# A ring of three tiles for v, loads held back, and no scores at the end of an h stage, in a fused attention and MLP kernel

## The chip, the cores and the metric

The kernel runs on one core of one Trainium2 chip. The metric is the device time of one execution in microseconds. Every time below is from runs on the chip; the engines are called PE (matmuls), ACT (activations), DVE (vector work), POOL (here the issuer of loads) and SP (the issuer of transposes and stores).

## What is computed

The reference, cut to what matters:

```python
batch, n_heads, seq, head_dim = 8, 12, 448, 64        # q, k, v
n_tokens, d_model, d_ff = 3584, 768, 2048             # w_in, w_out
scores = q @ k.T / sqrt(64) - log(448)
attn   = sigmoid(scores)                              # no softmax: no sums over rows
x      = (attn @ v), heads side by side               # 3584 x 768
h      = x @ w_in
out    = (h * sigmoid(h)) @ w_out
```

Inputs and output are float32 in HBM; the kernel works in float16 with float32 sums.

## The kernel before, in words

**Attention.** The 12 heads of a batch are worked four at a time, so there are 3 groups per batch and 24 groups g in all; group g belongs to batch g // 3. A group's q, k and v are loaded by `load` (L72): one tile [128, 2, 7, 64] float16 per tensor, in two transfers of 112 KB each, issued by POOL and converted from float32 on the way. Tiles come from rings: four for k, four for q, five for v. The load of a tile waits until the tile that had the slot before has been read by all its users, and POOL issues in program order, so a waiting load holds up all later ones.

q and k are needed transposed (`kT`, `qT`, rings of four). Groups 0 to 5 are transposed on PE (`pe_transpose`, L141). From group 6 on `dma_transpose` (L160) first copies the tile into rows (`kr`, `qr`; by ACT for groups 6 to 8, by DVE later), and SP then issues a DMA that transposes. `scores(g, ch)` (L171) does four 64x64 matmuls into one of two PSUM tiles `psc` and one sigmoid on ACT; seven of them make a group. `values(g)` (L195) does 28 matmuls with the group's v into two PSUM tiles `pav`, and DVE scales these into `xT`.

**MLP.** `h_unit(b, fc)` (L229) is one of 16 column blocks of a batch: six matmuls into a PSUM tile `ph`, a sigmoid on ACT (`tsig`), a product on DVE (`gTr`). 16 of them are an h stage. `out_set` (L286) makes two row blocks of the output with seven products of eight matmuls each instead of eight (sums and differences of the operands, `S1` to `S4` and `T1` to `T4`, are prepared on DVE). Its first product needs `gTr` of the lower eight column blocks, its second that of the upper eight, its third a difference of two blocks.

`ph`, `pav`, `po` (the products) and PE's transposes share a ring of four PSUM tiles, `ps_1`.

**Order.** The order is written by hand. `all_moe` (L376) is one long stream of MLP steps, each with a cost in ns (189 for a matmul of h, 163 for one of a product). The main loop takes two `scores` at a time ("a burst"), then `values` if a group is complete, then a row copy for a later group if one is due (`rows_if_any`), and then `stretch(ns)` (L395), which draws steps from the stream until their costs reach all that was granted so far. The grant per burst is 1600 to 3400 ns. Before burst 42 (group 6, first chunk) there is one long `stretch(21500)`, with no scores in it: the rest of batch 0's h stage, all of batch 1's and the start of the first `out_set`. In batch 1's h stage `by_h1` (L351) places the row copies and transposes of groups 6, 7 and 8 behind column blocks 4, 7 and 10, each followed by the loads of k and q four groups on.

Loads beside the first ones are issued from `after_transpose` (L425), `after_values` (L443), `by_h1` and `rows_if_any` (L461). `w_in` comes in four quarters (column blocks 4 to the quarter), `w_out` in four parts.

Of the kernel before, what the change touches and what calls it, by code (L numbers as in the profile page):

```python
# [17 lines left out]
def kernel(  # L18
# [21 lines left out]
    NFC = DFF // P  # L40
    NO2 = DMODEL // 2
    NQB = NQ * B
# [7 lines left out]
    p2 = ctx.enter_context(tc.tile_pool(name="p2", bufs=2))  # L50
    p3 = ctx.enter_context(tc.tile_pool(name="p3", bufs=3))
    p4 = ctx.enter_context(tc.tile_pool(name="p4", bufs=4))
    p5 = ctx.enter_context(tc.tile_pool(name="p5", bufs=5))
    p12 = ctx.enter_context(tc.tile_pool(name="p12", bufs=12))
    ps_sc = ctx.enter_context(tc.tile_pool(name="ps_sc", bufs=2, space=bass.MemoryType.PSUM))
    ps_1 = ctx.enter_context(tc.tile_pool(name="ps_1", bufs=4, space=bass.MemoryType.PSUM))
# [8 lines left out]
    flat = {}  # L65

    def new_flat(name, g):
        flat[name, g] = (p5 if name == "v" else p4).tile(
            [P, 2, NCH, D], F16, tag=f"{name}f", name=f"{name}f"
        )  # L70

    def load(names, g, c0=0, c1=NCH):  # L72
        b, iq = divmod(g, NQ)
        for name in names:
            if (name, g) not in flat:
                new_flat(name, g)
            for half in range(2):
                h0 = half * (H // 2) + 2 * iq
                nc.gpsimd.dma_start(  # L79
                    flat[name, g][half * HP : (half + 1) * HP, :, c0:c1].rearrange(  # L80
                        "p i c d -> p i (c d)"
                    ),
                    source[name][b, h0 : h0 + 2].rearrange("i (p c) d -> p i (c d)", c=NCH)[
                        :, :, c0 * D : c1 * D
                    ],
                )
# [20 lines left out]
    def load_w_in(step):  # L107
        cols = slice(step * DFF // 4, (step + 1) * DFF // 4)
        nc.gpsimd.dma_start(  # L109
            w_in_sb[:, :, cols], moe_w_in[:, cols].rearrange("(cc p) f -> p cc f", p=P)  # L110
        )

    def load_w_out(nh, part):
        cols = slice(nh * NO2, (nh + 1) * NO2)
        fcs = slice(part * NFC // 2, (part + 1) * NFC // 2)
        nc.gpsimd.dma_start(
            w_out_sb[:, fcs, cols],
            moe_w_out[part * DFF // 2 : (part + 1) * DFF // 2, cols].rearrange(
                "(fc p) e -> p fc e", p=P
            ),  # L120
        )
# [104 lines left out]

    pairs = [half * NQ + iq for iq in range(NQ - 1) for half in range(2)] + [NQ - 1, 2 * NQ - 1]

    def h_unit(b, fc):  # L229
        ph = ps_1.tile([P, 512], F32, tag="ps1", name="ph")  # L230
        for at, cc in enumerate(pairs):
            assert b in ready or at < 4
            nc.tensor.matmul(  # L233
                ph[:, :S],
                w_in_sb[:, cc, fc * P : (fc + 1) * P],
                xT[b][:, cc, :],
                start=(at == 0),
                stop=(at == NCC - 1),
            )
            if at < NCC - 1:  # L240
                yield 189
        if fc == NFC - 1:
            h_done.add(b)
        tsig = p3.tile([P, S], F16, tag="tsig", name="tsig")
        nc.scalar.activation(tsig, ph[:, :S], AF.Sigmoid, bias=0.0, scale=ISX)  # L245
        nc.vector.tensor_mul(  # L246
            gTr[:, fc, (b % 2) * S : (b % 2) * S + S], ph[:, :S], tsig
        )
        yield 189
# [34 lines left out]
        return [rows_of[2 * m + u // NCH, u % NCH] for u in (2 * g, 2 * g + 1)]  # L284

    def out_set(a1, rows1, a2, rows2, last=False):  # L286
        lo, hi = slice(0, NHC), slice(NHC, NFC)
        osb = [p4.tile([P, DMODEL], F32, tag="osb", name="osb") for _ in range(2)]
        c11, c12 = (osb[0][:, nh * NO2 : (nh + 1) * NO2] for nh in range(2))
        c21, c22 = (osb[1][:, nh * NO2 : (nh + 1) * NO2] for nh in range(2))  # L290
        m1 = p2.tile([P, NO2], F32, tag="m1", name="m1")
        sg = [cpool.tile([P, NHC, P], F16, tag=f"S{i}", name=f"S{i}") for i in range(1, 5)]

        def store(rows, o, cols, engines):
            for at, (row, eng) in enumerate(zip(rows, engines)):
                eng.dma_start(row[:, cols], o[at * HP : (at + 1) * HP, cols])

        left, right, whole = slice(0, NO2), slice(NO2, DMODEL), slice(0, DMODEL)

        def product(a, w):  # L300
            po = ps_1.tile([P, 512], F32, tag="ps1", name="po")
            for fc in range(NHC):
                nc.tensor.matmul(  # L303
                    po[:, :NO2], a[:, fc, :], w[:, fc, :], start=(fc == 0), stop=(fc == NHC - 1)
                )
                if fc < NHC - 1:
                    yield 163
            return po[:, :NO2]

        def plus(o, po, x, sign=ISX):  # L310
            nc.vector.scalar_tensor_tensor(  # L311
                out=o, in0=po, scalar=sign, in1=x, op0=ALU.mult, op1=ALU.add
            )

        nc.vector.tensor_sub(sg[2], a1[:, lo], a2[:, lo])  # L315
        nc.vector.tensor_add(sg[0], a2[:, lo], a2[:, hi])
        po = yield from product(a1[:, lo], wq[0][0])
        nc.scalar.activation(m1, po, AF.Copy, scale=ISX)  # L318
        nc.vector.tensor_sub(sg[1], sg[0], a1[:, lo])
        yield 163  # L320
        po = yield from product(a1[:, hi], wq[1][0])
        plus(c11, po, m1)
        nc.vector.tensor_sub(sg[3], a1[:, hi], sg[1])
        if last:
            store(rows1, osb[0], left, (nc.sync, nc.sync))
        yield 163
        po = yield from product(sg[2], tw[3])
        plus(c22, po, m1)
        yield 163
        po = yield from product(sg[1], tw[2])  # L330
        plus(c22, po, c22)
        plus(c12, po, m1)
        yield 163
        po = yield from product(a2[:, hi], tw[4])
        plus(c21, po, c22, -ISX)
        yield 163
        po = yield from product(sg[0], tw[1])
        plus(c22, po, c22)
        plus(c12, po, c12)
        store(rows2, osb[1], whole, (nc.sync, nc.sync))  # L340
        yield 163
        po = yield from product(sg[3], wq[1][1])
        plus(c12, po, c12)
        if last:
            store(rows1, osb[0], right, (nc.sync, nc.scalar))
        else:
            store(rows1, osb[0], whole, (nc.sync, nc.sync))
        yield 163


    by_h1 = {4: 6, 7: 7, 10: 8}  # L351
    early = [h_unit(0, fc) for fc in range(2)]
    sums = w_sums()

    def moe_h(b):
        for fc in range(NFC):
            yield from early[fc] if b == 0 and fc < 2 else h_unit(b, fc)
            if b == 1:
                if fc >= 2:
                    next(sums)  # L360
                if fc in by_h1:
                    for name in ("k", "q"):
                        dma_transpose(by_h1[fc], name, act_copy)
                    load("kq", by_h1[fc] + 4)

    def moe_set(m, g):
        step = out_set(block(g), row_blocks(m, g), block(g + 1), row_blocks(m, g + 1))
# [25 lines left out]
    done = due = 0.0  # L393

    def stretch(ns):  # L395
        nonlocal done, due
        due += ns
        while done < due:
            step_ns = next(stream, None)
            if step_ns is None:  # L400
                break
            done += step_ns
# [19 lines left out]
    units = [(g, ch) for g in range(NQB) for ch in range(NCH)]  # L422
    waiting = []

    def after_transpose(g):  # L425
        if g == 0:
            load("kq", 4)
            load_w_in(1)
        elif g == 1:
            load("kq", 5)  # L430
            load_w_in(2)
            load("v", 3)
            load_w_in(3)
            load("v", 4)
        elif g == 4:
            load("kq", 8)
            load("v", 6)
            load("v", 7)
        elif g == 5:
            load("v", 8)  # L440
            load("kq", 9)

    def after_values(g):  # L443
        if g == 0:
            load("v", 5)
            for nh in range(2):
                for part in range(2):
                    load_w_out(nh, part)
        elif g == 2:
            load("kq", 6)  # L450
            load("kq", 7)
        elif g >= 4 and g + 5 < NQB:
            load("v", g + 5)
        if g >= 6:
            for to in (9, 10) if g == 6 else (g + 4,):
                if to < NQB:
                    later.extend(((to, "k"), (to, "q")))

    later = []

    def rows_if_any():  # L461
        if later:
            g, name = later.pop(0)
            dma_transpose(g, name, nc.vector.tensor_copy)
            if name == "q" and g + 4 < NQB:
                load("kq", g + 4)

    def values_if_any():
# [110 lines left out]
```

## Time and profile before

| what | value |
| --- | --- |
| median of three runs | 386.41 us (384.43, 386.41, 386.48) |
| the profiled execution | 386.89 us |
| its span, first to last instruction | 385.1 us |
| around the span | 1.79 us |
| busy share of ACT, DVE, POOL | 62%, 61%, 24% |
| loads (POOL's queue) | 22.69 MB |
| stores and transposes (SP's queue) | 19.31 MB |

The share of busy time is an average over the whole span. PE's busy time counts matmuls whose ends are modelled, so what is worth looking for is not the share but the places at which PE had nothing to run, and what released it. In a line of the timeline the first number is the start in us from the span's start, the second the length of the run of instructions merged into that line, xN their count, and the bracket at the end the idle time of the engine ahead of it with its releaser. In a view of windows the columns are the stretch, its length, busy time of PE, PE's weight loads, DVE, ACT and POOL (counts in parentheses), the granted clock of PE, the busy share of the DMA engines and GB/s moved.

### The profile page before, as it was taken

What the parts mean: (1) busy time and instruction counts of PE and PEld (TensorE: products, weight loads), DVE (VectorE), ACT (ScalarE), POOL (GpSimd) and SP (SyncE); (2) the same over time, 40 slices, a digit from 0 to 9 for tenths busy, and PEclk for the clock granted to TensorE, in tenths of its full rate; (3) what the DMA queues carried; (4) which work ended last, traced back from release to release, by engine and by line L of the source; (5) the groups of instructions that cost most, each with busy time, mean ns of one, the idle gap of its engine ahead of it and who ended that gap; (6) DMA issues with size and microseconds to landing.
All of it is one profiled execution on the core that took longest, in us unless ns stands there. A gap on an engine that the chain in (4) does not pass through costs nothing.

```text
span 385.1 us, 7662 instructions
## 1 busy us (share of the span) xinstructions
PE 373.2 (97%) x3083; PEld 186.8 (48%) x3083; DVE 233.5 (61%) x415; ACT 240.1 (62%) x328; POOL 93.0 (24%) x158
## 2 busy tenths in 40 slices
PE   7998999997999999999999999999999999999995
PEld 2543445553544444444555444544455444555663
DVE  2445646894685656655767546745757444756774
ACT  4998685856766886678454587577874686044000
POOL 8953516541344313221312301101000000000000
PEclk9999999999999999999999999999999999999999
DMA  7999999999999999928949764445131300110233
GB/s 111 181 190 205 205 203 170 153 130 119 195 108 210 147 212 112 171 53 98 98 107 201 68 137 73 39 115 73 24 69 40 83 3 0 26 57 2 67 98 82
DMA packets 66403, 42.71 MB, mean 111 GB/s; under 512 B 37056, under 2 KB 62912, under 8 KB 66368
## 3 DMA queue, kind: packets, MB, share of 16 engines
q0 software_dynamic: 28032, 22.69, 45.0%
q1 hardware_dynamic: 38112, 19.31, 30.1%
q8 instruction: 24, 0.39, 0.4%
q10 hardware_dynamic: 224, 0.23, 0.2%
q14 instruction: 11, 0.09, 0.1%
HBM read 45.61 MB, written 11.01 MB: 147 GB/s over the span
## 4 chain that ended last, share of the span: by engine, by line
PE 83%; DMA 8%; ACT 5%; POOL 1%; issue 1%; DVE 1%; ACTq 0%; POOLq 0%
PE ph L233 36%; PE po L303 31%; PE psc L178 9%; PE pav L209 7%; ACT attnT L185 5%; DMA qT<-qr 4%; DMA vf<-in_v_dram 3%; DMA kf<-in_k_dram 1%; POOL qf L79 1%; DVE gTr L246 0%; ACT tsig L245 0%; PE ptrk L149 0%; POOL w_in_sb L109 0%; DVE S L315 0%; POOL vf L79 0%
## 5 line engine op out<-in xcount | busy, mean ns | idle before, releaser
L185 ACT ACTIVATE attnT<-psc,bias_s 128x896 f16<-128x896 f32 x168 | 159.1, 1015 | 57.7 <-PE psc L178 57.7
L233 PE MATMUL ph<-xT,w_in_sb 128*128 128x448 f16 x768 | 153.6, 353 | 0.0
L246 DVE TENSOR_TENSOR gTr<-ph,tsig 128x448 f16<-128x448 f32 x128 | 78.1, 623 | 75.3 <-ACT tsig L245 74.5
L233 PEld LDWEIGHTS <-w_in_sb 128*128 128x128 f16 x768 | 71.8, 98 | 76.2 <-issue 13.6
L245 ACT ACTIVATE tsig<-ph 128x448 f16<-128x448 f32 x128 | 68.2, 545 | 49.9 <-PE ph L233 49.0
L303 PEld LDWEIGHTS <-S 128*128 128x128 f16 x448 | 42.1, 98 | 34.5 <-issue 6.7
L79 POOL DMA_DIRECT2D vf<-in_v_dram x48 | 28.7, 615 | 104.7 <-PE pav L209 98.2
L311 DVE SCALAR_TENSOR_TENSOR osb<-po,osb 128x384 f32<-128x384 f32 x70 | 37.7, 555 | 26.7 <-PE po L303 26.1
L178 PE MATMUL psc<-qT,kT 64*64 64x448 f16 x672 | 50.4, 362 | 3.5 <-DMA qT<-qr 2.1
L220 DVE TENSOR_SCALAR xT<-pav 128x448 f16<-128x448 f32 x48 | 27.7, 620 | 30.9 <-PE pav L209 30.9
L303 PE MATMUL po<-T,S 128*128 128x384 f16 x224 | 40.7, 327 | 0.5 <-DVE S L315 0.5
L303 PEld LDWEIGHTS <-gTr 128*128 128x128 f16 x304 | 28.8, 98 | 23.5 <-issue 4.3
L303 PE MATMUL po<-w_out_sb,S 128*128 128x384 f16 x224 | 39.9, 326 | 0.0
L209 PE MATMUL pav<-attnT,vf 64*64 64x448 f16 x672 | 38.3, 350 | 1.7 <-DMA vf<-in_v_dram 1.2
L79 POOL DMA_DIRECT2D qf<-in_q_dram x48 | 28.8, 611 | 35.6 <-DVE qr L164 10.9
L303 PE MATMUL po<-w_out_sb,gTr 128*128 128x384 f16 x192 | 34.4, 326 | 0.2 <-DVE gTr L246 0.2
L79 POOL DMA_DIRECT2D kf<-in_k_dram x48 | 28.7, 606 | 20.5 <-DMA w_out_sb<-in_moe_w_out_dram 6.1
L178 PEld LDWEIGHTS <-kT 64*64 64x64 f16 x672 | 14.9, 104 | 34.1 <-issue 33.1
L209 PEld LDWEIGHTS <-vf 64*64 64x64 f16 x672 | 20.2, 107 | 14.0 <-DMA vf<-in_v_dram 1.9
L311 DVE SCALAR_TENSOR_TENSOR osb<-po,m 128x384 f32<-128x384 f32 x42 | 23.2, 552 | 3.5 <-PE po L303 3.1
L303 PE MATMUL po<-T,gTr 128*128 128x384 f16 x112 | 21.4, 326 | 0.0
L318 ACT ACTIVATE m<-po 128x384 f32<-128x384 f32 x14 | 6.9, 493 | 21.4 <-PE po L303 21.4
(40 smaller groups left out, 131.0 us busy)
## 6 DMA issues: line engine op xcount, KB each, us to landing
out_dram<-osb SPq DMA_DIRECT2D x54, 192.0 KB, 3.4
qf<-in_q_dram POOLq DMA_DIRECT2D x48, 112.0 KB, 7.3
vf<-in_v_dram POOLq DMA_DIRECT2D x48, 112.0 KB, 4.7
kf<-in_k_dram POOLq DMA_DIRECT2D x46, 112.0 KB, 7.6
w_in_sb<-in_moe_w_in_dram POOLq DMA_DIRECT2D x4, 768.0 KB, 10.8
w_out_sb<-in_moe_w_out_dram POOLq DMA_DIRECT2D x4, 768.0 KB, 15.3
kT<-kr SPq DMA_TRANSPOSE x18, 7.5
qT<-qr SPq DMA_TRANSPOSE x18, 7.0
```

Of the source, the lines that this page charges most:

```text
L79: nc.gpsimd.dma_start(flat[name, g][half * HP : (half + 1) * HP, :, c0:c1].rearrange("p i c d -> p i (c d)"), source[name][b, h0 : h0 + 2] ...
L178: nc.tensor.matmul(psc[own, j, :S], qkT["k", g][rows, ch, own], qkT["q", g][rows, :, own], start=True, stop=True,)
L185: nc.scalar.activation(attnT[g, ch], psc[:, :, :S], AF.Sigmoid, bias=bias_s, scale=QKSCALE)
L209: nc.tensor.matmul(pav[half][j * D : (j + 1) * D, :S], flat["v", g][own, j, ch, :], at[own, j, :], start=(ch == 0), stop=(ch == NCH - 1),)
L220: nc.vector.tensor_scalar_mul(xT[b][:, half * NQ + iq, :], pav[half][:, :S], SX)
L233: nc.tensor.matmul(ph[:, :S], w_in_sb[:, cc, fc * P : (fc + 1) * P], xT[b][:, cc, :], start=(at == 0), stop=(at == NCC - 1),)
L245: nc.scalar.activation(tsig, ph[:, :S], AF.Sigmoid, bias=0.0, scale=ISX)
L246: nc.vector.tensor_mul(gTr[:, fc, (b % 2) * S : (b % 2) * S + S], ph[:, :S], tsig)
L303: nc.tensor.matmul(po[:, :NO2], a[:, fc, :], w[:, fc, :], start=(fc == 0), stop=(fc == NHC - 1))
L311: nc.vector.scalar_tensor_tensor(out=o, in0=po, scalar=sign, in1=x, op0=ALU.mult, op1=ALU.add)
L318: nc.scalar.activation(m1, po, AF.Copy, scale=ISX)
```

## The change

It has four parts.

1. v's ring has three tiles instead of five. The load of v for group g+3 now stands behind `values(g)` throughout. v of group 3 (the first of batch 1) is issued ahead of the third quarter of `w_in`; v of group 4 behind the fourth quarter; v of group 5 between the halves of `w_out`.
2. The loads of v of groups 9 and 10 and of k and q of groups 10 to 12 are held: v of group 9 and then k and q of groups 10, 11 and 12, which hung on `by_h1`, are issued behind `values(6)`; v of group 10 follows `values(7)`. k and q of group 9 stand behind `values(5)`. From group 10 on the row copies of a group stand behind `values` of the group three earlier; before, it was four.
3. `by_h1` goes from blocks 4, 7, 10 to blocks 3, 6, 9.
4. `hold`: from the start of the last column block of an h stage (of any batch but 0) to the end of the first product of an `out_set`, `stretch` draws on beyond its grant, so that no burst falls into that stretch. What was drawn too much is drawn less in the next stretches.

```diff
-        flat[name, g] = (p5 if name == "v" else p4).tile(
+        flat[name, g] = (p3 if name == "v" else p4).tile(
...
     def h_unit(b, fc):
+        nonlocal hold
+        hold = b > 0 and fc == NFC - 1
...
         po = yield from product(a1[:, lo], wq[0][0])
         nc.scalar.activation(m1, po, AF.Copy, scale=ISX)
         nc.vector.tensor_sub(sg[1], sg[0], a1[:, lo])
+        hold = False
         yield 163
...
-    by_h1 = {4: 6, 7: 7, 10: 8}
+    by_h1 = {3: 6, 6: 7, 9: 8}
...
                     for name in ("k", "q"):
                         dma_transpose(by_h1[fc], name, act_copy)
-                    load("kq", by_h1[fc] + 4)
...
-        while done < due:
+        while done < due or hold:
...
     def after_transpose(g):
         if g == 0:
             load("kq", 4)
             load_w_in(1)
         elif g == 1:
             load("kq", 5)
-            load_w_in(2)
-            load("v", 3)
-            load_w_in(3)
-            load("v", 4)
         elif g == 4:
             load("kq", 8)
-            load("v", 6)
-            load("v", 7)
-        elif g == 5:
-            load("v", 8)
-            load("kq", 9)

     def after_values(g):
         if g == 0:
+            load("v", 3)
+            load_w_in(2)
+            load_w_in(3)
+        elif g == 1:
+            load("v", 4)
+            load_w_out(0, 0)
+            load_w_out(0, 1)
+        elif g == 2:
             load("v", 5)
-            for nh in range(2):
-                for part in range(2):
-                    load_w_out(nh, part)
-        elif g == 2:
+            load_w_out(1, 0)
+            load_w_out(1, 1)
             load("kq", 6)
             load("kq", 7)
-        elif g >= 4 and g + 5 < NQB:
-            load("v", g + 5)
-        if g >= 6:
-            for to in (9, 10) if g == 6 else (g + 4,):
-                if to < NQB:
-                    later.extend(((to, "k"), (to, "q")))
+        elif g + 3 < NQB:
+            load("v", g + 3)
+        if g == 6:
+            for to in (10, 11, 12):
+                load("kq", to)
+        if g == 5:
+            load("kq", 9)
+        if g >= 6 and g + 3 < NQB:
+            later.extend(((g + 3, "k"), (g + 3, "q")))
...
-            if name == "q" and g + 4 < NQB:
+            if name == "q" and g + 4 < NQB and g + 4 > 12:
                 load("kq", g + 4)
```

More of the change, by code (lines that the diff above doesn't have):

```diff
@@ L52 @@
     p4 = ctx.enter_context(tc.tile_pool(name="p4", bufs=4))
-    p5 = ctx.enter_context(tc.tile_pool(name="p5", bufs=5))
     p12 = ctx.enter_context(tc.tile_pool(name="p12", bufs=12))
@@ L286, in out_set @@
     def out_set(a1, rows1, a2, rows2, last=False):
+        nonlocal hold
         lo, hi = slice(0, NHC), slice(NHC, NFC)
@@ L319, in out_set @@
         nc.vector.tensor_sub(sg[1], sg[0], a1[:, lo])
+        hold = False
         yield 163
```

## The prediction

> **What bounds the kernel now.** I read the page first, then PE's waits, then PE's timeline at the places that the waits name, then POOL's and SP's timelines behind them, and the DMA in windows.
>
> ```profile
> span 385.1 us, 7662 instructions
> PE 373.2 (97%) x3083; PEld 186.8 (48%) x3083; DVE 233.5 (61%) x415; ACT 240.1 (62%) x328; POOL 93.0 (24%) x158
> ```
>
> PE is the bound: 11.9 us of the span are not covered by matmuls, and nothing but those, or PE work taken away, can be won. The change takes no PE work away. What ended PE's idle time (total us, times, longest):
>
> ```profile
> PE psc L178 <- DMA qT<-qr: 2.1, 1, 2.1
> ...
> PE pav L209 <- DMA vf<-in_v_dram: 1.2, 2, 1.0
> ...
> PE po L303 <- DVE S L315: 0.5, 2, 0.3
> ...
> PE po L303 <- DVE gTr L246: 0.2, 1, 0.2
> ```
>
> Two of these are transfers that come late: one transpose and one tile of v. Together they are most of what this change can reach. The rest of the idle time is the start of the kernel and the store at its end, which it does not touch. So the question is whether each late transfer comes in time, and whether another becomes late.
>
> **Part 1, the order of v3.** PE's timeline around `values(3)`, an undisturbed `values(5)` with the long h stretch behind it, and the DVE instruction that frees a PSUM tile for `values(3)`:
>
> ```profile
> 36.61 0.57 PE L178 MATMUL psc<-qT,kT 64*64 64x448 f16 x8
> 38.23 0.38 PE L209 MATMUL pav<-attnT,vf 64*64 64x448 f16 x2 [1.04 <-DMA vf<-in_v_dram]
> 38.80 1.51 PE L209 MATMUL pav<-attnT,vf 64*64 64x448 f16 x26 [0.20 <-DMA vf<-in_v_dram]
> 40.25 1.69 PE L233 MATMUL ph<-xT,w_in_sb 128*128 128x448 f16 x8
> ...
> 58.30 1.52 PE L209 MATMUL pav<-attnT,vf 64*64 64x448 f16 x28
> 59.75 18.90 PE L233 MATMUL ph<-xT,w_in_sb 128*128 128x448 f16 x99
> ```
>
> ```profile
> 36.54 0.62 DVE L246 TENSOR_TENSOR gTr<-ph,tsig 128x448 f16<-128x448 f32 x1 [0.48 <-ACT tsig L245]
> ```
>
> An undisturbed `values` takes 59.75 - 58.30 = 1.45 us to the next start. Without the wait for v3 the first matmul could go at about 37.2, since its PSUM tile is free when DVE has read block 4's `ph`, at 36.54 + 0.62 = 37.16. It would end at 38.65 instead of 40.25: **1.6 us** (the idle entries sum to 1.24; the rest is two matmuls that ran alone). Does v3 come by 37.2? POOL's timeline:
>
> ```profile
> 26.85 0.84 POOL L109 DMA_DIRECT2D w_in_sb<-in_moe_w_in_dram  x1
> 27.68 1.20 POOL L79 DMA_DIRECT2D vf<-in_v_dram  x2
> 31.80 0.85 POOL L109 DMA_DIRECT2D w_in_sb<-in_moe_w_in_dram  x1 [2.91 <-DMA w_in_sb<-in_moe_w_in_dram]
> ...
> 37.91 2.66 POOL L116 DMA_DIRECT2D w_out_sb<-in_moe_w_out_dram  x3 [2.88 <-DMA w_in_sb<-in_moe_w_in_dram]
> ...
> 49.27 0.59 POOL L79 DMA_DIRECT2D kf<-in_k_dram  x1 [3.15 <-DMA w_out_sb<-in_moe_w_out_dram]
> ...
> 60.57 0.59 POOL L79 DMA_DIRECT2D qf<-in_q_dram  x1 [3.04 <-DMA w_out_sb<-in_moe_w_out_dram]
> ```
>
> Counting the issues back, each of these waits ends when the transfer issued eight places earlier lands: 31.80 is the landing of w_in's second quarter, 37.91 of its third, 49.27 and 60.57 of the first and last part of w_out. So loads land in about the order of issue: three parts of w_out, 768 KB each, in 60.57 - 49.27 = 11.3 us, 204 KB per us. v3 today lies behind the third quarter. After the change it takes that quarter's place, behind group 5's k and q: 31.80 + 3 x 224 / 204 = **35.1**, 2.1 us ahead of need. At worst it lands when the larger third quarter did, 37.91, and PE waits 0.7 us: the gain lies between 0.9 and 1.6, and I take 1.6.
>
> ```profile
> 27.39 0.74 PE L209 MATMUL pav<-attnT,vf 64*64 64x448 f16 x12
> ...
> 42.88 1.88 PE L233 MATMUL ph<-xT,w_in_sb 128*128 128x448 f16 x9
> ```
>
> What is late next? The third quarter lands a tile later, 37.91 + 1.1 = 39.0; its first user is block 8, whose first matmul is the seventh of the nine at 42.88, so at 44.1, and 1.6 us earlier now: 42.5. v4 has the same bytes ahead of it as before. v5 moves behind two parts of w_out: 49.27 - 1.1 + 3.8 + 1.1 = 53.1, against `values(5)` at 58.30 - 1.6 = 56.7. The last part of w_out has the same bytes ahead too. The three slots do not bind: v3, v4 and v5 wait for `values(0)`, `(1)` and `(2)`, of which the last is over at 28.1, and POOL gets to v5 only when the fourth quarter is out, which still waits until 31.80. From group 9 on a load waits for `values` three groups earlier, is issued right behind them, and has three groups' time: nothing.
>
> **Part 2 and 3, the transpose of q7.** PE, the chain of waits, SP, ACT:
>
> ```profile
> 89.56 0.38 PE L178 MATMUL psc<-qT,kT 64*64 64x448 f16 x4
> 92.05 0.38 PE L178 MATMUL psc<-qT,kT 64*64 64x448 f16 x4 [2.11 <-DMA qT<-qr]
> ```
>
> ```profile
> 74.68 17.24 DMA qT<-qr
> ```
>
> ```profile
> 67.61 1.29 SPq L165 DMA_TRANSPOSE kT<-kr  x1
> ...
> 74.68 5.41 SPq L165 DMA_TRANSPOSE qT<-qr  x1
> ...
> 98.10 1.22 SPq L165 DMA_TRANSPOSE kT<-kr  x1
> 99.66 4.36 SPq L165 DMA_TRANSPOSE qT<-qr  x1
> ```
>
> ```profile
> 66.65 0.94 ACT L139 ACTIVATE kr<-kf 128x896 f16<-128x896 f16 x1
> ```
>
> The fourth transpose (q7) landed 92.05 - 67.61 = 24.4 us after the first was issued, 17.2 us after its own issue. The scores of group 7 want it at 92.05 - 2.11 = 89.9, and 1.6 us earlier, 88.3, once part 1 has its gain. `by_h1` moves the copies by one column block, 6 x 18.74 / 99 = 1.14 us (99 matmuls from 59.75 to 78.49); with part 1 the first issue is at 67.61 - 1.14 - 1.6 = 64.9. With 24.4 us as before the fourth lands at 89.3, 1.0 us late. That is one end. The other is no wait, if the DMA is faster. It was slow because loads ran beside it:
>
> ```profile
> 76.00:78.00 2.00, 2.00 (x13) 1.05 (x11) 2.00 (x5) 1.09 (x3) 1.15 (x2) 1.00 2.33 95
> 90.00:92.00 2.00, 0.00 (x0) 0.00 (x0) 0.00 (x0) 1.00 (x1) 1.06 (x2) 1.00 1.45 125
> 276.00:277.00 1.00, 1.00 (x12) 0.41 (x7) 0.62 (x2) 1.00 (x2) 0.00 (x0) 1.00 0.99 192
> ```
>
> A transpose alone (276) moves 192 GB/s; loads and transposes together 95 to 125. And which loads were these?
>
> ```profile
> 69.95 2.49 POOL L79 DMA_DIRECT2D vf<-in_v_dram  x4
> 73.28 0.59 POOL L79 DMA_DIRECT2D kf<-in_k_dram  x1 [0.84 <-DMA kf<-in_k_dram]
> ...
> 90.41 0.59 POOL L79 DMA_DIRECT2D kf<-in_k_dram  x1 [4.24 <-DMA kf<-in_k_dram]
> ```
>
> v9 and v10 at 69.95, then k10 from 73.28; by the same count of eight, the second half of k10 had landed at 90.41. These are the loads that the change holds until `values(6)`, 3.7 us earlier than in this row:
>
> ```profile
> 94.83 1.49 PE L209 MATMUL pav<-attnT,vf 64*64 64x448 f16 x28
> ```
>
> That is over at 92.6, about 93. At least v9, v10 and k10, 3 x 229 KB = 0.7 MB, leave the 24.4 us; at 125 GB/s that is 5.5 us, and a fifth of it is enough for the missing 1.0. I take the whole **2.1 us** (range 1.1 to 2.1). ACT's copy of k6 comes at 66.65 - 2.7 = 63.9 and q6's 0.9 later; k6 and q6 land behind w_out's last part, at 60.57 + 1.1 and + 2.2 = 62.8. This holds, by one microsecond; if it slips, only `tsig` slips with it, and ACT has half of each 1.14 us free there.
>
> **What part 2 brings nearer.** v9, k10 to k12 and, behind the row copies of group 9, k13 now go out in one bunch at about 93, 9 tiles or 2.06 MB, beside the transposes of group 9, which SP issues at 98.10 and 99.66 less 3.7. They are wanted by the last scores of the burst at
>
> ```profile
> 112.75 0.57 PE L178 MATMUL psc<-qT,kT 64*64 64x448 f16 x8
> ```
>
> less 3.7, plus 0.25: 109.3. That is 13.3 us after the second issue at 96.0. In the whole trace
>
> ```profile
> DMA to landing us min/median/max: 2.9/7.0/17.2
> ```
>
> is what qT took: the median leaves 6 us, the longest is 3.8 too long. I cost it at nothing, nearer the median since the queue of transposes is two deep here and was four deep at 17.2, and keep 3.8 for the range. For later groups a row copy still stands five or six bursts ahead of its scores, over 15 us. DVE's copy of k10 comes three bursts after its load is issued, about 9 us, against the median that the page gives for a k load:
>
> ```profile
> kf<-in_k_dram POOLq DMA_DIRECT2D x46, 112.0 KB, 7.6
> ```
>
> A DVE wait of a microsecond is covered by the four tiles of `ps_1`.
>
> **Part 4, hold.** Adding up the step costs against the grants, the burst order changes at four h stages: batches 2, 4, 5 and 6 (3 and 7 end without a burst in that stretch, 1 in the long one). Won are the waits at the end of batch 6's stage, in the rows above the 0.2 for gTr and the longest, 0.3, for S, **0.45** in all (the other wait for S, 0.2, is at batch 1's end and stays). Lost: the stretch after a held one is short. After batch 2 only 6 matmuls of a product, 6 x 163 ns = 1.0 us, stand between two bursts; 13, 11 and 9 after the others. A burst gives ACT two sigmoids:
>
> ```profile
> L185 ACT ACTIVATE attnT<-psc,bias_s 128x896 f16<-128x896 f32 x168 | 159.1, 1015 | 57.7 <-PE psc L178 57.7
> ```
>
> Two PSUM tiles are all that `psc` has, so a burst's second scores wait for the second sigmoid before them, about 0.4 + 2.0 us after the last burst began; with 0.5 + 1.0 + 0.25 they come 0.7 early after batch 2, and by 0 elsewhere (the nine after batch 6 are followed by no burst). **+0.7 us**; 0 if ACT has its head start, 2 if all places pay.
>
> **Sum.** -1.6 - 2.1 - 0.45 + 0.7 = -3.4 us on the profiled execution of 386.89 (span 385.1 and 1.8 around it): 383.5. By PE's waits it runs through from 92 to its end but for the 0.45, so a gain at 40 or 92 reaches the end. The median of the runs is 0.5 lower, 386.41, so I forecast **383.0**.
>
> **Rivals.** (a) The bunch at 93 makes group 9's transposes late. For it: 2.06 MB of loads and 0.46 MB of transposes at the 95 GB/s of the slowest window take 26 us, to 119, 9.8 us late. Against it: median latency, and transposes before them drained early. With the longest latency seen it costs 3.8 us (386.8), at the other bound 9.8 (392.8); I take 389. It decides against the change once q9 lands more than 13.3 + 3.4 = 16.7 us after its issue, and is slower by 0.5% from 18.6 us. [...] (b) The transpose of q7 still takes its 24.4 us because kT and qT delay one another and not the loads: 1.0 remains, 384.0. [...] (c) v3 comes no earlier than the third quarter did, since landing is not strictly in order: 0.7 of the 1.6 is lost and nothing else, 383.7; or it does not come earlier at all, 384.6. (d) hold costs the 2 us: 384.3.
>
> **Chances.** Forecast 0.62, (a) 0.10, (b) 0.12, (c) 0.09, (d) 0.07. The range reaches from all gains with no cost of hold (-4.15: 382.3), less 0.9 for the scatter of the runs of before (384.43 to 386.48), 381.4, to (a)'s longest latency seen, less the 0.5 between profiled run and median (386.4): about 0.85 of the cases. A measurement tells 0.5%, 1.9 us, from no change. Faster by more: all of the forecast but a tenth, (b), (d) and (c) for the most part, 0.73; same 0.18; slower 0.09, from (a).
>
> **What would show it.** In the profile after: no wait of `pav` for v near 37; `values(3)` ending at 38.7; transposes issued from about 65; no wait of `psc` for qT near 88; POOL waiting for PE from about 70 to 93; one wait of `psc` for ACT near 145, up to 0.7; no DVE wait ahead of the products of batch 6. Wrong would be a wait of `psc` for qT or kT near 109 or later, or of DVE for a k or q tile, longer than two microseconds.

## The result and the profile after

The changed kernel takes 382.56 us (median of six runs, 382.39 to 382.93), the kernel before 385.82 us in the runs beside it (384.43 to 386.48): a ratio of 0.992, 95% interval 0.990 to 0.994, or 3.0 us; the two medians differ by 3.3. The profiled execution fell from 386.89 to 382.75 us, 4.1 us. The ratios here and below leave disturbed runs out, as does the row of u_v3 below (one of its executions took 993 us), while the other medians and spans of runs are over all, so the two can differ a little.

The page's first lines, then all of PE's waits in the changed kernel (total us, times, longest):

```profile
span 381.0 us, 7663 instructions
...
PE 372.2 (98%) x3083; PEld 186.9 (49%) x3083; DVE 233.8 (61%) x415; ACT 240.0 (63%) x328; POOL 92.9 (24%) x158
```

```profile
PE pw L135 <- DVE bias_s L422: 1.5, 1, 1.5
PE psc L177 <- ACT attnT L184: 1.2, 4, 0.5
PE psc L177 <- DVE qT L155: 0.5, 1, 0.5
PE pav L208 <- DVE gTr L249: 0.4, 1, 0.4
```

No DMA stands among them any more. What is new is a fourth wait of `psc` for ACT, with 0.5 the longest. PE's timeline at the places of the prediction: `values(3)`, the first scores of groups 7 and 9, and the short stretch after batch 2's stage.

```profile
36.84 0.57 PE L177 MATMUL psc<-qT,kT 64*64 64x448 f16 x8
37.24 1.49 PE L208 MATMUL pav<-attnT,vf 64*64 64x448 f16 x28
38.67 1.69 PE L236 MATMUL ph<-xT,w_in_sb 128*128 128x448 f16 x8
...
87.85 0.57 PE L177 MATMUL psc<-qT,kT 64*64 64x448 f16 x8
...
108.73 0.57 PE L177 MATMUL psc<-qT,kT 64*64 64x448 f16 x8
...
143.78 0.38 PE L177 MATMUL psc<-qT,kT 64*64 64x448 f16 x4
144.64 0.38 PE L177 MATMUL psc<-qT,kT 64*64 64x448 f16 x4 [0.48 <-ACT attnT L184]
```

`values(3)` runs without a break and is over at 38.67, where before it was 40.25. The eight scores at 87.85, the last four of them group 7's first, run as one piece; before, these four stood 2.1 us behind. Those at 108.73, with group 9's among them, run as one piece too. POOL and SP:

```profile
26.87 1.20 POOL L78 DMA_DIRECT2D vf<-in_v_dram  x2
28.03 0.88 POOL L108 DMA_DIRECT2D w_in_sb<-in_moe_w_in_dram  x1
...
68.90 1.18 POOL L78 DMA_DIRECT2D qf<-in_q_dram  x2
92.64 1.18 POOL L78 DMA_DIRECT2D vf<-in_v_dram  x2 [22.56 <-PE pav L208]
```

```profile
64.90 1.30 SPq L164 DMA_TRANSPOSE kT<-kr  x1
...
95.64 1.36 SPq L164 DMA_TRANSPOSE qT<-qr  x1
```

v3 stands ahead of the third quarter; POOL waits from 70 to 92.64 for `values(6)`; the first transpose is issued at 64.90. And the DMA in windows:

```profile
80.00:82.00 2.00, 2.00 (x19) 1.05 (x19) 1.97 (x5) 1.55 (x2) 0.00 (x0) 1.00 0.75 164
82.00:84.00 2.00, 2.00 (x18) 0.93 (x17) 1.71 (x4) 1.35 (x3) 0.00 (x0) 1.00 0.00 0
```

From 82 the DMA has nothing to do: all six transposes of groups 6 to 8 are done, 6 us before the first scores of group 7. Taken one by one, q7's transpose landed 8.8 us after its issue, at 80.8; q9's 6.6 us after, at 102.2; and v3 at 34.6, where 35.1 was forecast.

### The profile page after: what moved, and what is told of

Its sections match the earlier page's. It is cut to its first block, busy times and chain, and to the rows that moved or that the text cites. A ratio compares the mean times of both kernels' runs of the same rounds, so it can differ in the third digit from the quotient of the medians.

```text
span 381.0 us, 7663 instructions
## 1 busy us (share of the span) xinstructions
PE 372.2 (98%) x3083; PEld 186.9 (49%) x3083; DVE 233.8 (61%) x415; ACT 240.0 (63%) x328; POOL 92.9 (24%) x158
## 4 chain that ended last, share of the span: by engine, by line
PE 80%; DMA 12%; DVE 2%; ACT 2%; POOL 1%; issue 1%; DVEq 0%
PE po L307 34%; PE ph L236 29%; PE psc L177 9%; PE pav L208 6%; DMA w_in_sb<-in_moe_w_in_dram 6%; DMA w_out_sb<-in_moe_w_out_dram 5%; DVE gTr L249 1%; DMA ks<-in_k_dram 1%; ACT attnT L184 1%; DMA vf<-in_v_dram 1%; DVE T L278 1%; POOL qf L78 1%; PE pw L135 1%; POOL kf L78 0%; ACT qr L138 0%
## 5 line engine op out<-in xcount | busy, mean ns | idle before, releaser
L307 PEld LDWEIGHTS <-gTr 128*128 128x128 f16 x304 | 28.7, 98 | 23.4 <-issue 5.2
```

The lines of the kernel that those rows point to most:

```text
L307: nc.tensor.matmul(po[:, :NO2], a[:, fc, :], w[:, fc, :], start=(fc == 0), stop=(fc == NHC - 1))
```

## The experiments

Each kernel differs from the changed kernel or from the one before by the few lines shown. Times are medians with the range of the runs; the ratio is against the kernel before on the same chip. Not all runs were on one chip: beside them the median of the kernel before was 386.08 (u_v3, u_ring5, u_by_h1, held_alone), 385.46 (after_again, u_hold, hold_b6, by_h1_alone), 385.43 (v3_alone, u_v3_again), 385.57 (u_v3_fill) and 385.68 (rows9_late), so a difference between medians of different groups is uncertain by some 0.6 us.

| run | differs from | median, us (runs, range) | ratio, 95% interval | PE's waits for DMA, us |
| --- | --- | --- | --- | --- |
| after_again | the changed kernel itself | 382.63 (12, 382.11 to 384.42) | 0.993, 0.990 to 0.995 | none for v or qT |
| u_v3 | change, v3 behind the quarter | 384.21 (9, 383.13 to 386.71) | 0.994, 0.991 to 0.998 | no profile of use |
| u_v3_again | the same | 384.62 (10, 383.19 to 386.77) | 0.996, 0.993 to 1.000 | v 1.1 |
| u_v3_fill | u_v3 with filling | 384.38 (12, 383.92 to 385.39) | 0.996, 0.994 to 0.999 | v 0 (filled) |
| u_ring5 | change, five tiles of v | 382.53 (10, 382.19 to 383.79) | 0.992, 0.989 to 0.994 | none for v or qT |
| u_by_h1 | change, by_h1 as before | 382.91 (10, 382.33 to 383.41) | 0.993, 0.990 to 0.995 | none for v or qT |
| v3_alone | before, v3 ahead | 383.60 (10, 382.63 to 384.84) | 0.994, 0.991 to 0.998 | qT 1.0 |
| held_alone | before, loads held | 384.79 (10, 383.32 to 387.78) | 1.000, 0.996 to 1.003 | v 1.6 |
| by_h1_alone | before, by_h1 as changed | 384.64 (10, 383.63 to 388.43) | 0.999, 0.996 to 1.003 | v 2.3 |
| u_hold | change, no hold | 382.71 (12, 382.46 to 383.80) | 0.994, 0.991 to 0.996 | none for v or qT |
| hold_b6 | change, hold for batch 6 only | 381.89 (6, 381.69 to 382.26) | 0.991, 0.987 to 0.994 | none for v or qT |
| rows9_late | change, copies two bursts later | 385.12 (10, 383.81 to 388.96) | 1.002, 0.998 to 1.006 | qT 1.4 |

**v of group 3.**

```diff
         if g == 0:
-            load("v", 3)
             load_w_in(2)
+            load("v", 3)
             load_w_in(3)
```

> The change with one thing undone: v of group 3 is issued behind w_in's third quarter again. Theory (the order of issue is the order of landing): PE waits for v at values(3) as before, 1.2 us in the waits view, and values(3) ends 1.6 us later than the 38.67 of the changed kernel; the time is 1.6 us above the changed kernel's 382.6, about 384.2. Everything behind moves by the same 1.6. Rival (POOL's earlier issue of everything behind it, not the order of these two, made v early): no wait for v, 382.6.

> The same kernel as in the run with v of group 3 behind w_in's third quarter, again, for a profile (the first one's profiled execution took 993 us, disturbed by something outside). Theory: a wait of pav for v at values(3) of one to two us, no wait for qT, time 384.2, with a scatter of some us between runs like that of before.

Measured: 384.21 and 384.62, 1.6 and 2.0 above the 382.6 of the changed kernel. Each taken against the kernel before beside it, they gain 1.9 and 0.8 where the changed kernel gains 3.3 and 2.8 (after_again), so undoing this one swap costs 1.0 to 2.5. In the second run's profile PE's waits have v back:

```profile
PE pav L208 <- DMA vf<-in_v_dram: 1.1, 2, 1.0
```

So the order of these two issues decides whether PE waits; the rival falls. But the runs are spread over 3.6 us, and those of the changed kernel mostly over less than one.

**v of group 3 alone, and the wait for q7.** The same swap made in the kernel before, and nothing else:

```diff
             load("kq", 5)
-            load_w_in(2)
             load("v", 3)
+            load_w_in(2)
             load_w_in(3)
```

> The kernel before with one thing changed: v of group 3 is issued ahead of w_in's third quarter. Everything else as before, by_h1 at 4, 7, 10, loads of v9, v10 and k and q of groups 10 to 12 beside the transposes, no hold. Theory: no wait for v at values(3); transposes from 66.0, the fourth lands up to 24.4 us later at 90.4, scores want it at 88.3: the wait of psc for qT stays, about 2 us; time 1.6 below before, about 384.1 where before is 385.7. The run that undid only by_h1, with the loads held, had no such wait; that pair tells whether the held loads alone remove it. Rival (the wait for qT in the profile of before was chance, and v alone is the gain): no wait for qT, 382.9.

Measured: 383.60, where theory had 384.1 and the rival 382.9. The wait for qT is there, half as long as in the profile of before. PE and SP in this run:

```profile
87.93 0.38 PE L178 MATMUL psc<-qT,kT 64*64 64x448 f16 x4
89.35 0.38 PE L178 MATMUL psc<-qT,kT 64*64 64x448 f16 x4 [1.04 <-DMA qT<-qr]
```

```profile
65.99 1.29 SPq L165 DMA_TRANSPOSE kT<-kr  x1
```

The fourth transpose landed 89.35 - 65.99 = 23.4 us after the first was issued, with the same loads beside it as before, when it was 24.4. What the rest of the change, hold included, is worth beyond v3 is thus 383.60 - 382.6 = 1.0 us (1.0 to 1.4 against the kernel before beside each; the intervals of the two ratios overlap).

**Which part removes that wait.** Undone from the change one at a time: the ring of three (which alone stops POOL), and the earlier copies.

```diff
+    p5 = ctx.enter_context(tc.tile_pool(name="p5", bufs=5))
...
-        flat[name, g] = (p3 if name == "v" else p4).tile(
+        flat[name, g] = (p5 if name == "v" else p4).tile(
```

> The change with one number undone: v's ring has five tiles again, all issue orders as changed. Theory: the ring of three is what holds the loads of v9, v10 and k and q of groups 10 to 12, since POOL issues in order and only v9's wait for values(6) stops it; with five tiles POOL issues v9 and what stands behind it at about 70 again, they share the DMA with the transposes of groups 6 to 8, the DMA stays busy through 82 to 88 instead of idling, and the transpose of q7 lands up to 24.4 us after the first issue at 64.9, that is at 89.3, 1.0 us late: a wait of psc for qT of 0 to 1.0 us, time 382.6 to 383.6. Rival (the transposes delay one another, loads do not matter): transposes done by 82 as in the changed kernel, 382.6, no load beside them missed.

```diff
-    by_h1 = {3: 6, 6: 7, 9: 8}
+    by_h1 = {4: 6, 7: 7, 10: 8}
```

> The change with one thing undone: row copies of groups 6, 7 and 8 behind column blocks 4, 7 and 10 again. Theory (the held loads alone made room): transposes are issued from 66.0 instead of 64.9 and are all done by about 83, long before scores of group 7 at 88.1: no wait of psc for qT, 382.6, the same as the changed kernel. Rival (the earlier place was needed): a wait of 1.1 us or more, 383.7.

Measured: 382.53 and 382.91, no wait for qT in either. With five tiles the loads do go out beside the transposes, and the DMA does not come to rest. POOL, then the windows:

```profile
72.94 1.32 POOL L79 DMA_DIRECT2D vf<-in_v_dram  x2 [0.67 <-DMA vf<-in_v_dram]
74.86 1.21 POOL L79 DMA_DIRECT2D kf<-in_k_dram  x2 [0.60 <-ACT tsig L249]
```

```profile
82.00:84.00 2.00, 2.00 (x19) 1.06 (x19) 1.71 (x4) 1.56 (x2) 0.56 (x1) 1.00 0.91 97
```

So the ring is what holds the loads, as the theory has it, and yet one column block of a head start was enough without it.

When q7's transpose landed tells how near it was. From issue to landing it took 17.2 us in the profile of before, 14.6 in v3_alone, 14.9 in u_ring5 and 15.7 in by_h1_alone below, all with the loads beside it; with the loads held it took 8.8 in the changed kernel (11.4 in after_again, 11.8 in hold_b6, the longest), 7.9 in u_by_h1 and 2.9 in held_alone below. v3_alone and u_by_h1 are the plainest pair: the first transpose is issued at 65.99 and 66.05, and what else differs acts earlier or later. So the loads are what makes it late. In held_alone the six transposes, issued one behind the other from 69.41, had all landed after 11.0 us, so they do not hold one another up for 24. In u_ring5 q7 landed at 86.4 and was wanted at 87.5, 1.1 us to spare, and with the 17.2 of the profile of before it would have been late; in u_by_h1 6.5 us were to spare. In these executions each part by itself suffices; the held loads are what makes the margin wide. The two were also added to the kernel before one at a time:

> Of the change only the ring of three with the loads held behind values(6) (and the later place of the row copies that goes with it); v3 behind w_in's third quarter, by_h1 at 4, 7, 10, no hold of scores. Theory: the wait for v at values(3) is there (1.2 us), the one for qT of group 7 is gone: before less 2.3, 383.5 where before is 385.8. Rival (the earlier place of the copies is needed as well): 1.0 or more of the wait stays, 384.5 to 385.8.

> The kernel before with one thing changed: row copies, transposes and the loads four groups on behind blocks 3, 6, 9. Theory (loads beside the transposes set the rate; they move along with the copies): the transpose of q7 lands 1.1 us earlier, the wait of psc for qT shrinks from 2.1 to about 1.0, 384.7 where before is 385.8. Rival (the place of the copies is what counts, as the transposes delay one another): as much or more, the wait gone, 383.7. Third possibility: the loads that move up with them fill the DMA earlier and nothing is won, 385.8.

The first is the changed kernel with three lines undone (the swap of v3, `by_h1`, `hold = False`), the second changes only the line of `by_h1`. Measured: 384.79 and 384.64. Neither profile has a wait for qT, which is what theory expected of the first, and more than it expected of the second. In time they cannot be told from the kernel before by the ratio (1.000 and 0.999, each within 0.4%); their medians are 1.3 and 0.8 below those of the kernel before beside them. So held_alone missed the 383.5 of its theory and lies where its rival had it, although the wait that the rival kept is not there, and the gain from the wait for qT alone is not shown in time. Both keep the wait for v, and it was long in their profiled executions (1.6 and 2.3 us). What that wait does, the first one shows. PE's timeline, then the windows (the granted clock is the third number from the end):

```profile
38.39 0.38 PE L208 MATMUL pav<-attnT,vf 64*64 64x448 f16 x2 [1.40 <-DMA vf<-in_v_dram]
38.96 2.58 PE L208 MATMUL pav<-attnT,vf 64*64 64x448 f16 x26 [0.19 <-DMA vf<-in_v_dram]
41.47 2.26 PE L236 MATMUL ph<-xT,w_in_sb 128*128 128x448 f16 x8
```

```profile
38.00:39.00 1.00, 0.41 (x6) 0.15 (x10) 0.00 (x0) 0.77 (x1) 0.62 (x2) 1.00 1.25 208
39.00:40.00 1.00, 1.00 (x16) 0.58 (x20) 0.00 (x0) 0.00 (x0) 1.00 (x2) 0.63 1.24 207
40.00:41.00 1.00, 1.00 (x18) 0.40 (x10) 0.00 (x0) 0.00 (x0) 0.48 (x1) 0.50 1.25 203
41.00:42.00 1.00, 1.00 (x8) 0.28 (x3) 0.78 (x2) 0.00 (x0) 0.00 (x0) 0.50 1.27 200
42.00:43.00 1.00, 1.00 (x6) 0.40 (x3) 0.38 (x1) 0.55 (x1) 0.00 (x0) 0.66 1.29 202
```

The 26 matmuls that take 1.51 us in the profile of before take 2.58 here, and the eight behind them 2.26 instead of 1.69. The granted clock is 0.5 for (1 - 0.63)/0.5 + 2 + (1 - 0.66)/0.5 = 3.4 us: half of that, 1.7 us, is lost behind the wait and on top of it. In by_h1_alone the same is seen from 40 to 44 (0.73, 0.50, 0.50 and 0.56 in windows of 1 us), again 3.4 us. In the profile of before, and in u_v3_again, whose row this is,

```profile
40.00:42.00 2.00, 2.00 (x24) 0.88 (x23) 1.42 (x4) 1.19 (x3) 0.00 (x0) 1.00 1.26 200
```

the clock stays at 1.00 behind waits of 1.2 and 1.1.

**Is it the clock that scatters the runs?** u_v3 once more, with PE kept busy in most of the wait:

```diff
+        if g == 3:
+            for _ in range(6):
+                nc.tensor.matmul(pav[0], dummy[:, :P], dummy, start=True, stop=True)
         for ch in range(done_rounds, end):
```

> The kernel with v of group 3 behind w_in's third quarter, with six matmuls of no use (into the PSUM tile that values(3) then overwrites) put in front of values(3), so that PE is busy for 1.3 of the about 1.7 us in which it waits for v. Theory (the scatter of the kernels that wait comes from the granted clock, which fell to 0.5 for some 3 us behind the wait in two of the profiles and stayed at 1.0 in two others): the wait stays as long, but the clock stays at 1.0 and the slow runs go: all or nearly all runs between 383.1 and 384.9, where the two runs without the filling had 7 of 19 from 385.3 to 386.8; median about 384.0. Rival (the scatter is v landing at different times): median and scatter as without the filling, 384.3 to 384.6 and up to 386.8.

Measured: 384.38, with a range of 383.92 to 385.39. Without the filling 7 of 19 runs were from 385.3 to 386.8, with it 1 of 12 is, at 385.39. The timeline:

```profile
37.58 1.47 PE L205 MATMUL pav<-dummy 128*128 128x512 f16 x6
38.98 1.64 PE L211 MATMUL pav<-attnT,vf 64*64 64x448 f16 x28
```

The upper end of the scatter is gone, as the theory has it, and so is the lower: the six useless matmuls take their 1.4 us however early v comes, so the best runs are 0.7 later and the median does not fall to 384.0 but is where the rival had it.

The mean granted clock that is listed for each execution says more. A stretch of 3.4 us at half clock takes 1.7 / 385 = 0.0044 off it. Of the 19 executions without the filling six have 0.995 or 0.996, and these are the six slowest, 386.3 to 386.8; the other 13 have 0.997 or more and take 383.1 to 385.3. With the filling none of the 12 is below 0.997. Of the executions of the kernels that wait for v (u_v3, u_v3_again, held_alone, by_h1_alone) 12 of 39 have 0.996 or less, of rows9_late, which waits 1.4 us for qT, 4 of 10, and of all other changed kernels here none of 78. Of the kernel before, 27 of 109 have it, with a median of 387.9 against 385.1 for the others. So the loss of clock makes most of the uppermost times; the rest of the scatter (383.0 to 387.9 in those 82) has other causes, and a mean does not say behind which wait the clock fell.

**hold.** Undone, and confined to batch 6, beside the changed kernel itself:

> The changed kernel once more, as the mark for the kernels beside it: 382.6.

```diff
-        hold = b > 0 and fc == NFC - 1
+        hold = False
```

> The change without hold: bursts may fall into the end of an h stage again. Theory (hold gives 0.45 at the end of batch 6 and takes 0.67 after batch 2): 0.2 faster than the changed kernel, 382.4; the profile has waits of po for gTr and S near 322 (0.2 and 0.3) and none of psc for ACT near 144. Rival (hold is worth its 0.45 and the short stretch costs nothing, since ACT's waiting work is done later anyway): 383.0.

```diff
-        hold = b > 0 and fc == NFC - 1
+        hold = b == 6 and fc == NFC - 1
```

> The change with hold for batch 6 only. Theory: keeps the 0.45 and does not pay the 0.67 after batch 2: 381.9, 0.7 below the changed kernel. Rival as in the run without hold: no difference, 382.6.

Measured: 382.63, 382.71, 381.89. Confined to batch 6, hold saves 382.71 - 381.89 = 0.8; the other batches cost 382.63 - 381.89 = 0.7; as changed it is worth 0.1, within the scatter. PE without hold, at the end of batch 6's stage:

```profile
322.13 0.34 PE L307 MATMUL po<-w_out_sb,gTr 128*128 128x384 f16 x1 [0.19 <-DVE gTr L249]
322.73 0.34 PE L307 MATMUL po<-T,S 128*128 128x384 f16 x1 [0.26 <-DVE S L319]
```

and PE's waits for ACT with hold for batch 6 only, one fewer and 0.4 less than in the changed kernel:

```profile
PE psc L177 <- ACT attnT L184: 0.8, 3, 0.4
```

The run without hold came out between theory (382.4) and rival (383.0) and does not decide between them; the one for batch 6 is the theory's 381.9. It is the fastest kernel of all: five of its six runs lie below all twelve of the changed kernel beside them, though the intervals of the two ratios overlap.

**How near the bunch of loads was.**

```diff
+        if g == 6:
+            later.extend(((None, None), (None, None)))
         if g >= 6 and g + 3 < NQB:
...
             g, name = later.pop(0)
+            if name is None:
+                return
```

> The changed kernel with the row copies of group 9 (and so all copies queued behind them, and the loads that follow copies) two bursts later. This tries the rival of the prediction, the bunch of loads behind values(6), by taking 5 us from its margin: the transpose of q9 is then issued at about 100.8 and its scores come at 109.0, 8.2 us later. The longest landing of qT in the changed kernel's profile is 11.5 us, the median 6.2. Theory (the bunch is no danger, the margin was 5 us or more): no wait of psc for qT, 382.6. Rival (the change stands at the edge): a wait of up to 3.3 us near 109, up to 385.9.

Measured: 385.12, 2.5 above the changed kernel, and a wait. PE, then SP:

```profile
108.25 0.38 PE L177 MATMUL psc<-qT,kT 64*64 64x448 f16 x4
110.07 0.38 PE L177 MATMUL psc<-qT,kT 64*64 64x448 f16 x4 [1.44 <-DMA qT<-qr]
```

```profile
102.72 1.22 SPq L164 DMA_TRANSPOSE qT<-qr  x1
```

The transpose of q9 was issued 7.1 us later than in the changed kernel, not the 5.1 that I expected, and landed 7.4 us after its issue. The theory's "no danger with 5 us less" is therefore not tried by it; what it shows is that with 7 us less the wait is there. The runs scatter up to 389, as those of held_alone and by_h1_alone do (387.8 and 388.4); the four slowest have a mean clock of 0.991 to 0.996.

## Why the prediction was right, step by step

The forecast was 383.0, the range 381.4 to 386.4, and the time is 382.56; the direction and the mechanisms held. By its steps:

- **v3's order.** Right in place and in the profile's size: `values(3)` was to end at 38.65 and ends at 38.67. Over many runs undoing it costs 1.6 to 2.0 by the medians, but that is a mixture: of the executions without the swap, those that keep their clock are some 1.2 above the changed kernel, and the six that lose it some 3.8. The loss of clock was not in the sum.
- **The transpose of q7.** The wait went, as forecast; its term was sized at 2.1 from one execution, and the runs give 1.0 for it and hold together (v3_alone against the changed kernel), so about 0.9. The profiled execution of before was one with a long wait, and its 386.89 against a median of 385.8 fits that. The bound of 1.0 us late, without help from the loads, took 24.4 us as fixed; it was 23.4 in v3_alone, and with the head start of one block there was no wait even with the loads beside (u_ring5). That loads slow the transposes is borne out: q7's took 14.6 to 17.2 us with them beside it and 2.9 to 11.8 with them held, and the six of held_alone took 11.0 us in all, which also rules out rival (b), that the transposes delay one another. The 95 to 125 GB/s that the prediction gives for both together are two of the windows only: from 68 to 88 the windows of 2 us in the profile of before run from 90 to 183.
- **The bunch behind `values(6)`**, the rival on the slower side. POOL issued it at 92.64 (about 93 was forecast), and q9's transpose at 95.64 against scores at 108.73 + 0.25, the 13.3 us of the prediction. It landed 6.6 us after its issue, near the median of 7.0 that the prediction leaned on. rows9_late makes the mechanism real: it decides once about half of that margin is gone.
- **hold.** Both terms held: 0.7 lost after batch 2, seen as 0.48 of idle time at 144.64 and a burst broken in two, and 0.45 or a little more won at batch 6. Net 0.25 lost was forecast; 0.1 won was measured, within the scatter.
- **Sum.** Forecast -3.4: measured -3.0 in the runs beside it, -4.1 between the two profiled executions. The parts measured apart, 1.6 to 2.0 for v3 and 1.0 for q7 and hold together, make 2.6 to 3.0. That the forecast came within 0.5 us is in part luck: q7's term was twice too large, hold's was 0.35 too pessimistic, the loss of clock was left out, and the median of 386.41 from which it started was that of three runs, 0.6 above that of the six beside the result. One slip is in the range: (a)'s 386.8 already stood on the forecast of 383.0, and the 0.5 between profiled run and median was taken off it again.

Left open: why the same four transposes took 24.4 us in one execution and 23.4 in another, and whether it was at `values(3)` that the 27 of 109 executions of before lost their clock; both would need profiles of many executions. What removing the wait for q7 gains by itself in time is open too: the profiles show the wait gone, but held_alone and by_h1_alone show no gain clear of the noise.

## What to carry to other kernels

Where PE is 97% busy, read the few waits behind the share: each names its transfer, and moving one issue in POOL's order past a larger one was worth more, by the medians, than the rest of the change (1.6 to 2.0 us against 1.0). A part of a change can be worth its gain at one place and lose the same at another: hold paid at one stage end of four, and restricting it to that one gave another 0.7 us. A wait of PE must be costed with what its clock does afterwards: here 1.7 us came on top of waits of 1.6 and 2.3 us (held_alone, by_h1_alone) and nothing on top of those of 1.1 and 1.2 (u_v3_again, before). So the profile of one execution can show too little; the mean granted clock of every run shows how often it happens.

## What the runs showed of the hardware

A PE wait of 1.6 us (1.40 and 0.19, in two pieces, held_alone) and one of 2.3 us (by_h1_alone) were each followed by 3.4 us at a granted clock of 0.5, as worked out above from the windows of 1 us. Waits of 1.0 (v3_alone), 1.1 (u_v3_again), 1.2 (before) and 1.4 us (rows9_late) were not, nor was one of 2.1 us, at 90 in the profile of before: there the clock stayed at 1.00. So the length of the wait alone does not decide it. What does is not shown: the same kernel is hit in some runs only (in u_v3 and u_v3_again 6 of 19 have a mean clock of 0.995 or 0.996), and no run here moves a wait in time and leaves its length.

A transpose alone moved 192 GB/s (276 to 277 in the profile of before); with several issued one behind the other, and POOL's last load issued 4 us earlier, the DMA moved 277 GB/s (74 to 76 in held_alone). Beside loads both together moved 90 to 183 GB/s in windows of 2 us (68 to 88 in the profile of before), and a transpose took up to 17.2 us from issue to landing (q7), against 2.9 for the one issued at 274.61 with no load beside it; in the changed kernel the longest landing of qT was 11.5 us.
